# Another order of emission for the seven-product down steps of a spectral-filter and bilinear-GLU kernel

## The chip, the core and the metric

The kernel runs on one NeuronCore of a Trainium2 chip. The metric is the device time of one execution in microseconds (us). The engines are named as the profile names them: PE (TensorE matmul) with PEld (its weight loads), DVE (VectorE), ACT (ScalarE), POOL (GpSimd) and SP, whose queue issues most DMAs. Each engine works through its own list of instructions in order and waits on semaphores for the others.

## The reference

```python
x = A_x                                            # 1 x 2048 x 640
h = x + irfft2(rfft2(layernorm(x)) * (w_r + 1j * w_i))
z = layernorm(h)
g = z @ w_gate; u = z @ w_up                       # 640 x 1728 each
h2 = h + (g * u) @ w_down                          # 1728 x 640
```

All values are fp32. The change touches only the last two lines.

## The kernel before

Every fp32 operand of a matmul is split into a high part (a rounded copy, made on ACT) and a low part (the difference, made on DVE or POOL), and a product is three matmuls: high by high, high by low, low by high. Each engine's order is the order in which the code emits instructions; nothing reorders them.

The first part of the kernel (to about 190 us) is the spectral filter. The GLU part then runs over two blocks of 1024 tokens. The 1728 columns of the gate and up weights are cut into 14 chunks; a down step `p` takes two chunks. In a block, step 6 comes first (the last two chunks, computed plainly by `gu` and `gate_parts`), then steps 0 to 5. At the start of block 1 the normalised tokens are turned by PE transposes (`transp` for tiles 8 to 15, `fifth` for the last 128 columns of four tiles at once), and between them the last down step of block 0 is finished (`down`).

Steps 0 to 5 run `strassen` once for each of their two chunks. I call the two calls of a step its first and its second pass. A pass forms the gate and up products of one chunk by seven block products instead of eight: `product` issues groups of three matmuls (`triple`) into the PSUM banks `p11`, `acc_a` and `p53` (buffers `e` in the profile; there are four, used in turn). Partial results are copied out by ACT (`p1`, `u2`, `m5`) while PE works at another bank, and an accumulation onto `acc_a` or `p53` has to wait until its copy is done. Two quadrants of the gate product come out: `h[0](p53, m5)` and, at the end, `h[1](acc_a, p1)`.

In block 1, steps 0 to 4 are "mixed": their down product is also formed by seven block products. For it the quadrants of both passes are added and subtracted into seven operands, `unit(0)` to `unit(6)`, each with a high part (`high_of`, ACT) and a low part (`low_of`, DVE, for units 3 and 4 POOL). `mixed_first` makes units 2 and 3 at the end of the first pass, `mixed_second` units 0, 4, 5, 1 and 6 at the end of the second. `pending` is a list of such pieces that are put off, and `flush` emits them. `load_mixed` loads the down weights and gives three pieces: high parts of the plain weights; their low parts and the weight sums on POOL; and high and low parts of the sums (`third`, which is `wdn[2]`).

`mixed_down` turns the seven down products of step `p` into 16 stages, which are woven into the first pass of step `p + 1`: `tick` emits one stage after each group of three matmuls, from `p11` on. I call such a pass woven (its list `fine` is not empty; there are five, of steps 1 to 5). The stages of two token tiles alternate:

```python
k == 0:  unit 2 x b11                         then one DVE add of that bank (both line 911)
k == 1:  unit 4 x t2 onto it, unit 5 x t1     then one DVE add of both banks (line 904)
k == 2:  unit 3 x t3, unit 6 x b22            the same
else:    unit 0 x t4, unit 1 x b21            the same
```

`ahead` holds four pieces that prepare the gate and up weights of the next pass: `copies` (line 702 on ACT, 703 on POOL), `sums` (706 to 709 on POOL), `high` (714 on ACT) and `low` (719 on POOL). When `low` is through, the next load into the staging tile `raw` can start. `side` holds pieces by place, which `at(n)` emits.

Of the kernel before, what the change touches and what calls it, by code (L numbers as in the profile page):

```python
# [13 lines left out]
AF = mybir.ActivationFunctionType  # L14
OP = mybir.AluOpType
# [31 lines left out]
def tile_spectral_glu(ctx: ExitStack, tc: tile.TileContext, x, wf, wgu, wlast, wdown, wdlast,  # L47
                      cc, ci, fmain, frem, imain, irem, mm, out):
    nc = tc.nc
# [6 lines left out]
    tt, act = nc.vector.tensor_tensor, nc.scalar.activation  # L56
# [160 lines left out]
    def at(base, t):  # L217
        return view(base, 4 * t, [[64, 32], [1, 4]])
# [370 lines left out]
    def transp(t):  # L589
        turn_mm(t)  # L590
        turn_hi(t)
        turn_lo(t)
# [134 lines left out]
    def high_of(u, src):  # L727
        act(unit(u)[0], src, AF.Copy)  # L728

    def low_of(u, src, engine=nc.vector):  # L730
        hi, lo = unit(u)
        engine.tensor_tensor(lo, src, f32(hi), op=OP.subtract)  # L732
# [45 lines left out]
    def issue(job, parts=(0, 1)):  # L778
        for i in parts:
            for h in job[i]:  # L780
                h()

    EX, RAW, pending = {}, {}, []

    def flush():
        while pending:
            pending.pop(0)()

    def raw(k):
        RAW[k] = work.tile([P, 512], F32, tag="raw", name="rawh", bufs=3)  # L790
        return RAW[k]
# [10 lines left out]
    def mixed_first():  # L802
        def h1(ps, m):
            tt(raw(21), ps, m, op=OP.mult)
            return lambda: None

        def h0(ps, m):
            tt(ps, ps, m, op=OP.mult)
            high_of(2, ps)
            tt(raw(3), ps, RAW[21], op=OP.subtract)  # L810
            high_of(3, RAW[3])

            def rest():
                low_of(2, ps)
                low_of(3, RAW[3], nc.gpsimd)
            return rest
        return h1, h0

    def mixed_second():
        def h1(ps, m):  # L820
            tt(ps, ps, m, op=OP.mult)
            high_of(0, ps)
            tt(raw(2), ps, RAW[3], op=OP.subtract)
            high_of(4, RAW[2])

            def rest():
                low_of(0, ps)
                low_of(4, RAW[2], nc.gpsimd)
                tt(ps, ps, RAW[21], op=OP.add)
                high_of(5, ps)  # L830
                pending.append(lambda: low_of(5, ps))
            return rest

        def h0(ps, m):
            tt(ps, ps, m, op=OP.mult)
            high_of(1, ps)
            flush()

            def rest():
                low_of(1, ps)  # L840
                tt(ps, ps, RAW[2], op=OP.subtract)
                high_of(6, ps)
                pending.append(lambda: low_of(6, ps))
            return rest
        return h1, h0

    def load_mixed(p):
# [79 lines left out]
    def strassen(c, blk, h, ahead, downs, side, fine=()):  # L927
        wa, ws = W[c]
        fine = list(fine)

        def some(n):
            for _ in range(n):
                if downs:
                    downs.pop(0)()
                    pop(1)

        def at(n):
            for f in side.get(n, ()):
                f()

        def tick():
            if fine:
                fine.pop(0)()

        b11, b21, b22 = ([operand(sb, k + i) for i in range(2)] for sb, k in ((0, 0), (0, 2), (1, 2)))
        t1, t2 = ([(TJ["12"][:, 0, m, k], TJ["12"][:, 1, m, k]) for k in range(2)] for m in range(2))
        t4 = [operand(1, k) for k in range(2)]
        b5 = [operand(sb, 4) for sb in range(2)]
        p11, acc_a, p53 = single(), single(), single()

        def product(o, w, a, ms, extra=(), start=True, tick=tick):
            triple(o, [(w, a + P * i, m) for i, m in enumerate(ms)] + list(extra), start, tick)

        product(acc_a, wa, 384, b11, tick=None)
        p1, u2, m5 = (wk([P, 512], n) for n in ("p1", "u2", "m5"))
        act(p1, acc_a, AF.Copy)  # L956
        at(0)
        product(p11, wa, 0, b21, [(wa, 256, b5[0])])
        if ahead:
            ahead[0]()  # L960
            ahead[1]()
        flush()
        tt(p1, p11, p1, op=OP.add)
        at(1)
        product(acc_a, ws, 0, t2, start=False)
        act(u2, acc_a, AF.Copy)
        if ahead and fine:
            ahead[2]()
            ahead[3]()
            ahead = None  # L970
        product(p53, ws, 256, t1, [(wa, 896, b5[1])])
        act(m5, p53, AF.Copy)  # L972
        some(2)
        at(2)
        product(acc_a, ws, 640, [(t3[:, k, 0], t3[:, k, 1]) for k in range(2)], start=False)
        tt(m5, acc_a, m5, op=OP.add)  # L976
        some(1)
        product(p53, ws, 896, b22, [(ws, 512, b5[1])], start=False)
        tt(p53, p53, u2, op=OP.add)
        rest = h[0](p53, m5)  # L980
        at(3)
        some(2)
        rest()
        if ahead:
            ahead[2]()
            ahead[3]()
        product(acc_a, wa, 640, t4, [(wa, 896, b5[0])], start=False)
        while fine:
            tick()
        some(1)  # L990
        rest = h[1](acc_a, p1)
        at(4)
        some(1)
        rest()
        some(8)
        at(5)
# [5 lines left out]
    for n, (blk, p) in enumerate(steps):  # L1002
        if p == 6:
            s13, s12 = count % 3, (count + 1) % 3
            if blk == 0:
                load_raw(0)
                copies, sums, high, low = prep(0, blk, nc.vector)
                TJ["12"] = home("qr", [P, 2, 2, 2, 512], "t12", F32R)
                t1s = [t12(j) for j in range(4)]
                for j in range(4):  # L1010
                    t1s[j][0]()
                copies()
                t1s[0][1]()
                late()
                t1s[1][1]()
                t1s[2][1]()
                fifth((5, 6, 7))
                t1s[3][1]()
                late = gate_parts(NC - 2, 0, s12)
                sums()  # L1020
                high()
                for j in range(4):
                    t_rest(j)
                hi, lo = t34(0)
                hi()
                low()
                lo()
                late()
                gu(NC - 1, 1)
                wdn = load_d(p)  # L1030
                gate_parts(NC - 1, 1, s13)()
            else:
                copies, sums, high, low = prep(0, blk)
                js = [4, 5, 6, 7, 0, 1, 2, 3]
                for j in range(8):
                    transp(8 + j)
                    if j % 4 == 3:
                        fifth(range(5 + j, 9 + j))
                    if j >= 1:
                        down(*prev, js[j - 1], True)  # L1040
                    if j == 3:
                        copies()
                        sums()
                    if j == 5:
                        high()
                        low()
                down(*prev, js[7], True)
                gu(NC - 1, 0)
                gate_parts(NC - 1, 0, s13)()
                gu(NC - 2, 0)  # L1050
                TJ["12"] = home("qr", [P, 2, 2, 2, 512], "t12", F32R)
                t1s = [t12(j) for j in range(4)]
                late = gate_parts(NC - 2, 0, s12)
                for j in range(4):
                    t1s[j][0]()
                    t_rest(j)
                late()
                gu(NC - 1, 1)
                for j in range(4):
                    t1s[j][1]()  # L1060
                wdn = load_d(p)
                late = gate_parts(NC - 1, 1, s13)
                hi, lo = t34(0)
                hi()
                late()
                lo()
            gu(NC - 2, 1)
            gate_parts(NC - 2, 1, s12)()
            issue(wdn)
            prev = (blk, 6, [(2 * k, 2 * k + 1) for k in (s12, s13)])  # L1070
            count += 2
            load_raw(1)
            if blk == 0:
                fs, cs = scale_shift(range(8, 16), None)
                fill.extend(fs + cs)
            continue
# [14 lines left out]
        for ci in range(2):  # L1091
# [1 line left out]
            side = {}  # L1093
            ahead = None
            if c == 0:
                side[0] = t34(1)
            if c < 11:
                ahead = prep(c + 1, blk)
                side[5] = [lambda c=c: load_raw(c + 2)] if c < 10 else []
            if ci == 0 and mixed:  # L1100
                side[2] = [wdn[0], wdn[1]]
                side[4] = [wdn[2]]
            elif ci == 0:
                side[3] = [lambda wdn=wdn: issue(wdn)]
            if c == 11 and blk == 0:
# [148 lines left out]
```

## Time and profile before

| what | value |
|---|---|
| median of 3 runs | 747.57 us (746.79 to 748.72) |
| profiled execution | 750.67 us, its span 748.5 us, mean granted PE clock 0.981 |
| PE busy | 708.4 us (95%) |
| DVE, ACT, POOL busy | 446.5, 293.0 and 334.9 us (60%, 39%, 45%) |
| woven passes begin (their first stage) | 513.63, 556.57, 601.65, 646.28, 690.89 us |

The span runs from the first to the last instruction; 2.2 us of the execution lie around it. In the timeline a row is: start, duration (of all that are merged in it), engine, line, operation, out<-in, how many, and in brackets how long the engine had been idle and what released it.

### The profile page before, as it was taken

To read this page: it belongs to the slowest core of one execution; us is meant where nothing else is said; L and a number is where in the kernel's file an instruction comes from. 1 tells how busy PE (TensorE), PEld (TensorE's weight loads), DVE (VectorE), ACT (ScalarE), POOL (GpSimd) and SP (SyncE) were. 2 spreads that over 40 slices of the span, in tenths; PEclk is the share of its full clock that TensorE was granted. 3 is DMA by queue.
4 is the path that set the end of the run, shared out by engine and by line. 5 is a ranking of instruction groups with operands and counts; after the bars stand their busy time and mean duration, and the time that the engine had idled before them with its cause. 6 is when DMAs were issued, how large, how long until landed. Compare 5 with 4: busy or idle time off the path is not lost.

```text
span 748.5 us, 10074 instructions
## 1 busy us (share of the span) xinstructions
PE 708.4 (95%) x3832; PEld 621.3 (83%) x3832; DVE 446.5 (60%) x787; ACT 293.0 (39%) x554; POOL 334.9 (45%) x310
## 2 busy tenths in 40 slices
PE   7899998999999999999999999999979888898898
PEld 6788997887788989898888888897968777797887
DVE  7968886897964444454434475655645365564554
ACT  4756665375443223232232473533142232324220
POOL 3301114331165545545464521475776656575610
PEclk9999999999999999999999999999999999899999
DMA  9305663001201211121112122212103020110203
GB/s 338 150 8 191 224 214 127 1 1 44 96 3 36 71 35 71 36 71 36 70 36 89 39 102 100 77 36 70 36 0 106 1 71 35 56 51 0 71 0 141
DMA packets 20927, 55.04 MB, mean 74 GB/s; under 512 B 2320, under 2 KB 6928, under 8 KB 20880
## 3 DMA queue, kind: packets, MB, share of 16 engines
q1 hardware_dynamic: 20304, 52.70, 20.2%
q0 software_dynamic: 288, 1.48, 0.6%
q8 instruction: 30, 0.49, 0.3%
q10 hardware_dynamic: 288, 0.23, 0.1%
q14 instruction: 17, 0.14, 0.1%
HBM read 49.16 MB, written 5.24 MB: 73 GB/s over the span
## 4 chain that ended last, share of the span: by engine, by line
PE 72%; DVE 17%; ACT 6%; issue 2%; DMA 1%; POOL 1%; DVEq 0%; ACTq 0%
PE e L82 36%; PE y L82 24%; PE re L82 2%; PE im L82 2%; PE u L341 2%; PE eo L82 2%; ACT ht L728 2%; DVE fold L191 1%; ACT wst L714 1%; DVE fold L196 1%; DVE ht L732 1%; PE im L391 1%; PE im L390 1%; PE ir L382 1%; ACT wd L860 1%
## 5 line engine op out<-in xcount | busy, mean ns | idle before, releaser
L82 PE MATMUL e<-xt,wst 128*128 128x512 f32 x864 | 214.7, 391 | 2.6 <-ACT m L972 1.4
L82 PEld LDWEIGHTS e<-xt,wst 128*128 128x128 f32 x864 | 159.1, 188 | 32.7 <-ACT m L972 1.7
L82 PE MATMUL y<-wd,ht 128*128 128x320 f32 x1048 | 175.3, 315 | 11.4 <-DVE x L911 9.3
L82 PEld LDWEIGHTS y<-wd,ht 128*128 128x128 f32 x1048 | 164.2, 192 | 22.0 <-issue 11.4
L703 POOL TENSOR_TENSOR wst<-raw,wst 128x1024 fp32r<-128x1024 f32 x24 | 59.8, 2492 | 108.0 <-ACT wst L702 108.0
L508 DVE TENSOR_TENSOR x<-y,x 128x640 f32<-128x640 f32 x79 | 64.9, 823 | 68.0 <-PE y L82 67.8
L728 ACT ACTIVATE ht<-e 128x512 fp32r<-128x512 f32 x47 | 28.1, 598 | 176.6 <-DVE e L796 100.0
L82 PE MATMUL e<-t,wst 128*128 128x512 f32 x288 | 80.3, 424 | 9.0 <-ACT p L956 9.0
L82 PEld LDWEIGHTS e<-t,wst 128*128 128x128 f32 x288 | 58.2, 207 | 22.4 <-ACT p L956 11.4
L719 POOL TENSOR_TENSOR wst<-raw,wst 128x896 fp32r<-128x896 f32 (+1 forms) x46 | 64.8, 1432 | 23.6 <-ACT wst L714 23.6
L904 DVE TENSOR_TENSOR x<-y,x 128x640 f32<-128x640 f32 x60 | 49.4, 824 | 38.6 <-PE y L82 38.6
L464 POOL TENSOR_TENSOR wd<-draw,wd 128x640 fp32r<-128x640 f32 x18 | 28.0, 1579 | 66.7 <-ACT wd L463 66.7
L976 DVE TENSOR_TENSOR m<-e,m 128x512 f32<-128x512 f32 x24 | 16.5, 689 | 59.1 <-PE e L82 57.8
L702 ACT ACTIVATE wst<-raw 128x1024 fp32r<-128x1024 f32 x24 | 25.4, 1060 | 48.4 <-DMA raw<-in_wgu_dram 48.4
L82 PE MATMUL e<-xt,wdir 128*128 128x512 f32 x180 | 41.9, 392 | 1.1 <-DVE q L494 1.1
L732 DVE TENSOR_TENSOR ht<-e,ht 128x512 fp32r<-128x512 f32 x47 | 32.2, 684 | 17.3 <-ACT ht L728 16.9
L714 ACT ACTIVATE wst<-raw 128x896 fp32r<-128x896 f32 (+1 forms) x48 | 30.0, 676 | 29.2 <-POOL raw L708 28.4
L82 PEld LDWEIGHTS e<-xt,wdir 128*128 128x128 f32 x180 | 33.4, 188 | 8.3 <-ACT xt L547 1.3
L82 PE MATMUL e<-ht,wst 128*128 128x512 f32 x144 | 37.7, 391 | 0.0
L207 PE MATMUL im<-bits,fold 128*128 128x128 f32 x192 | 29.9, 292 | 6.7 <-DVE fold L196 2.3
L409 POOL CAST qr<-bits 1x128 fp32r<-1x128 f32 x16 | 4.5, 281 | 68.0 <-DVE qr L406 68.0
L207 PEld LDWEIGHTS im<-bits,fold 128*128 128x128 f32 x192 | 24.6, 193 | 11.4 <-DVE fold L196 5.6
(210 smaller groups left out, 1167.4 us busy)
## 6 DMA issues: line engine op xcount, KB each, us to landing
raw<-in_wgu_dram SPq DMA_DIRECT2D x24, 640.0 KB, 3.9
wts<-in_wf_dram SPq DMA_DIRECT2D x16, 644.0 KB, 4.0
draw<-in_wdown_dram SPq DMA_DIRECT2D x24, 320.0 KB, 4.6
x<-in_x_dram SPq DMA_DIRECT2D x16, 320.5 KB, 6.0
out_dram<-x SPq DMA_DIRECT2D x15, 320.0 KB, 2.2
bits<-in_mm_dram SPq DMA_DIRECT2D x32, 128.0 KB, 4.0
raw<-in_wgu_dram SPq DMA_DIRECT2D x4, 320.0 KB, 4.0
draw<-in_wdlast_dram SPq DMA_DIRECT2D x4, 320.0 KB, 2.9
```

Source lines behind the costliest of these rows:

```text
L82: nc.tensor.matmul(o, l, r, start=start, stop=stop, skip_group_check=True)
L207: nc.tensor.matmul(pm[:, k * P:(k + 1) * P], l, c, start=n == 0, stop=n == len(ls) - 1)
L464: los.append(lambda r=r, a=a, b=b: engine.tensor_tensor(w[:, 1, a:b], r, f32(w[:, 0, a:b]), op=OP.subtract))
L508: tt(xv, ps[:, :, 0:320], xv, op=OP.add)
L702: act(wa[:, 0], stage[:, 0:1024], AF.Copy)
L703: nc.gpsimd.tensor_tensor(wa[:, 1], stage[:, 0:1024], f32(wa[:, 0]), op=OP.subtract)
L714: act(ws[:, 0, o:o + b - a], stage[:, a:b], AF.Copy)
L719: ptt(ws[:, 1, o:o + b - a], stage[:, a:b], f32(ws[:, 0, o:o + b - a]), op=OP.subtract)
L728: act(unit(u)[0], src, AF.Copy)
L732: engine.tensor_tensor(lo, src, f32(hi), op=OP.subtract)
L904: tt(xv, PQ[q][:, :, 0:320], xv, op=OP.add)
L976: tt(m5, acc_a, m5, op=OP.add)
```

## The change

The sums of gate products, the low parts and the weight sums are emitted in another order:

- `flush(n)` emits at most n pieces instead of all.
- `mixed_first`: only the multiplication and the subtraction for unit 3 stand at the end of the first pass. The two high and two low parts of units 2 and 3 are put off into the second pass: one behind its `p1` copy, two between `copies` and `sums`, one behind `sums`.
- `mixed_second`: the subtraction for unit 4 goes ahead of the high part of unit 0; the sum of unit 5 goes behind the multiplication of the second quadrant; the low parts of units 5, 1 and 6 and the sum of unit 6 are put off. In the woven pass one such piece follows each stage.
- In a woven pass, `copies` and `sums` come behind the `u2` copy (before: behind `p11`), `high` and `low` behind the `m5` copy (before: ahead of it).
- The high and low parts of the weight sums (`wdn[2]`) come ahead of the last quadrant's work of the first pass (`at(6)`), before behind it (`at(4)`).
- The down weights of step 6 are split inside the next pass, behind its `p1` copy, before ahead of that pass.
- At the start of block 1, `fifth` comes behind the down step that it stood ahead of, twice.

```diff
-    def flush():
-        while pending:
-            pending.pop(0)()
+    def flush(n=8):
+        for h in pending[:n]:
+            h()
+        del pending[:n]
...
         def h0(ps, m):                       # mixed_first
             tt(ps, ps, m, op=OP.mult)
-            high_of(2, ps)
             tt(raw(3), ps, RAW[21], op=OP.subtract)
-            high_of(3, RAW[3])
-            def rest():
-                low_of(2, ps)
-                low_of(3, RAW[3], nc.gpsimd)
-            return rest
+            pending.extend([
+                lambda: high_of(2, ps),
+                lambda: low_of(2, ps),
+                lambda: high_of(3, RAW[3]),
+                lambda: low_of(3, RAW[3], nc.gpsimd)])
+            return lambda: None
...
         def h1(ps, m):                       # mixed_second
             tt(ps, ps, m, op=OP.mult)
+            tt(raw(2), ps, RAW[3], op=OP.subtract)
             high_of(0, ps)
-            tt(raw(2), ps, RAW[3], op=OP.subtract)
             high_of(4, RAW[2])
-            def rest():
+            low_of(4, RAW[2], nc.gpsimd)
+            def fifth_sum():
                 low_of(0, ps)
-                low_of(4, RAW[2], nc.gpsimd)
                 tt(ps, ps, RAW[21], op=OP.add)
                 high_of(5, ps)
                 pending.append(lambda: low_of(5, ps))
-            return rest
+            held.append(fifth_sum)
+            return lambda: None
...
         def h0(ps, m):                       # mixed_second
             tt(ps, ps, m, op=OP.mult)
             high_of(1, ps)
-            flush()
-            def rest():
-                low_of(1, ps)
+            held.pop()()
+            def sixth_sum():
                 tt(ps, ps, RAW[2], op=OP.subtract)
                 high_of(6, ps)
-                pending.append(lambda: low_of(6, ps))
-            return rest
+            pending.extend([lambda: low_of(1, ps), sixth_sum, lambda: low_of(6, ps)])
+            return lambda: None
...
             if fine:                         # tick
                 fine.pop(0)()
+                flush(1)
...
+        woven = bool(fine)                   # strassen
         product(acc_a, wa, 384, b11, tick=None)
...
         at(0)
+        if not woven:
+            flush(1)
         product(p11, wa, 0, b21, [(wa, 256, b5[0])])
-        if ahead:
+        if ahead and not woven:
             ahead[0]()
+            flush(2)
             ahead[1]()
-        flush()
+            flush()
         tt(p1, p11, p1, op=OP.add)
         at(1)
         product(acc_a, ws, 0, t2, start=False)
         act(u2, acc_a, AF.Copy)
-        if ahead and fine:
+        flush()
+        if ahead and woven:
+            ahead[0]()
+            ahead[1]()
+        product(p53, ws, 256, t1, [(wa, 896, b5[1])])
+        act(m5, p53, AF.Copy)
+        if ahead and woven:
             ahead[2]()
             ahead[3]()
-            ahead = None
-        product(p53, ws, 256, t1, [(wa, 896, b5[1])])
-        act(m5, p53, AF.Copy)
...
         some(1)
+        at(6)
         rest = h[1](acc_a, p1)
...
                     transp(8 + j)            # start of block 1
+                    if j >= 1:
+                        down(*prev, js[j - 1], True)
                     if j % 4 == 3:
                         fifth(range(5 + j, 9 + j))
-                    if j >= 1:
-                        down(*prev, js[j - 1], True)
...
-            issue(wdn)
+            first_wd = wdn
...
-                side[0] = t34(1)
+                side[0] = [*t34(1), lambda j=first_wd: issue(j)]
...
-                side[4] = [wdn[2]]
+                side[6] = [wdn[2]]
```

On ACT, at the seam between the first and the second pass of step 2 (`p` is the copy `p1` of the second pass, `wd` the high parts of the weight sums, line 728 a high part of a unit), there stood:

```order
L860 ACTIVATE ex_4066<-draw_4364 128x640
L728 ACTIVATE ht_1714<-e_4368 128x512
L728 ACTIVATE ht_1714<-rawh_4561 128x512
L860 ACTIVATE wd_4362<-draw_4363 128x640
L860 ACTIVATE wd_4362<-draw_4364 128x640
L956 ACTIVATE p1_4580<-e_4572 128x512
L702 ACTIVATE wst_4593<-raw_1814 128x1024
```

and now stands:

```order
L862 ACTIVATE ex_4062<-draw_4360 128x640
L862 ACTIVATE wd_4358<-draw_4359 128x640
L862 ACTIVATE wd_4358<-draw_4360 128x640
L960 ACTIVATE p1_4576<-e_4568 128x512
L728 ACTIVATE ht_1714<-e_4364 128x512
L702 ACTIVATE wst_4590<-raw_1814 128x1024
L728 ACTIVATE ht_1714<-rawh_4564 128x512
```

Both high parts of the units moved behind `p1`, and the weight sums' high parts are now ahead of everything that waits for the last quadrant.

On DVE, at the seam between the second pass of step 2 and the woven first pass of step 3 (835, now 838, is the second quadrant's multiplication; 829, now 831, the sum of unit 5; 841, now 843, that of unit 6; 911 and 904, now 913 and 906, the stages' adds; 963, now 970, the `p1` sum), there stood:

```order
L823 TENSOR_TENSOR rawh_4637<-e_4573,rawh_4561 128x512
L732 TENSOR_TENSOR ht_1714<-e_4573,ht_1714 128x512
L829 TENSOR_TENSOR e_4573<-e_4573,rawh_4527 128x512
L835 TENSOR_TENSOR e_4572<-e_4572,p1_4580 128x512
L732 TENSOR_TENSOR ht_1714<-e_4573,ht_1714 128x512
L732 TENSOR_TENSOR ht_1714<-e_4572,ht_1714 128x512
L841 TENSOR_TENSOR e_4572<-e_4572,rawh_4637 128x512
L911 TENSOR_TENSOR x1_67<-y_4685,x1_67 128x320
L911 TENSOR_TENSOR x1_67<-y_4693,x1_67 128x320
L904 TENSOR_TENSOR x1_67<-y_4685,x1_67 128x2x320
L732 TENSOR_TENSOR ex_4066<-e_4572,ex_4066 128x512
L963 TENSOR_TENSOR p1_4678<-e_4669,p1_4678 128x512
```

and now stands:

```order
L838 TENSOR_TENSOR e_4568<-e_4568,p1_4576 128x512
L732 TENSOR_TENSOR ht_1714<-e_4569,ht_1714 128x512
L831 TENSOR_TENSOR e_4569<-e_4569,rawh_4527 128x512
L913 TENSOR_TENSOR x1_67<-y_4681,x1_67 128x320
L732 TENSOR_TENSOR ht_1714<-e_4569,ht_1714 128x512
L913 TENSOR_TENSOR x1_67<-y_4690,x1_67 128x320
L732 TENSOR_TENSOR ht_1714<-e_4568,ht_1714 128x512
L906 TENSOR_TENSOR x1_67<-y_4681,x1_67 128x2x320
L843 TENSOR_TENSOR e_4568<-e_4568,rawh_4636 128x512
L970 TENSOR_TENSOR p1_4674<-e_4665,p1_4674 128x512
L906 TENSOR_TENSOR x1_67<-y_4690,x1_67 128x2x320
L732 TENSOR_TENSOR ex_4062<-e_4568,ex_4062 128x512
```

The first stage's add moved ahead of three operations that make units 5, 1 and 6, and the low part of unit 6 (`ex`) moved behind the `p1` sum and one more stage's add.

On PE, at the start of block 1 (537 is a transpose of `transp`, 568 one of `fifth`, `y` a down step), the difference is:

```order
 L537 MATMUL e<-ident,zt 128x128 x4
+L82 MATMUL y<-wd,ht 128x320 x12
 L568 MATMUL e<-ident,zt 128x128 x4
-L82 MATMUL y<-wd,ht 128x320 x12
 L537 MATMUL e<-ident,zt 128x128 x4
 L82 MATMUL y<-wd,ht 128x320 x12
```

One down step of 12 matmuls moved ahead of the four transposes.

More of the change, by code (lines that the diff above doesn't have):

```diff
@@ L808, in h0 @@
             tt(ps, ps, m, op=OP.mult)
-            high_of(2, ps)
             tt(raw(3), ps, RAW[21], op=OP.subtract)
-            high_of(3, RAW[3])
-            def rest():
-                low_of(2, ps)
-                low_of(3, RAW[3], nc.gpsimd)
-            return rest
+            pending.extend([
[4 more added lines that the diff above has]
+            return lambda: None
         return h1, h0
     def mixed_second():
+        held = []
         def h1(ps, m):
             tt(ps, ps, m, op=OP.mult)
+            tt(raw(2), ps, RAW[3], op=OP.subtract)
             high_of(0, ps)
-            tt(raw(2), ps, RAW[3], op=OP.subtract)
             high_of(4, RAW[2])
-            def rest():
+            low_of(4, RAW[2], nc.gpsimd)
+            def fifth_sum():
                 low_of(0, ps)
-                low_of(4, RAW[2], nc.gpsimd)
                 tt(ps, ps, RAW[21], op=OP.add)
@@ L983, in strassen @@
         rest()
-        if ahead:
+        if ahead and not woven:
             ahead[2]()
```

## The prediction

> **What bounds the kernel now.** The first view is the page's list of busy times:
>
> ```profile
> PE 708.4 (95%) x3832; PEld 621.3 (83%) x3832; DVE 446.5 (60%) x787; ACT 293.0 (39%) x554; POOL 334.9 (45%) x310
> ```
>
> PE is the bound almost everywhere, and the change takes no matmul away. So there is something to win only where PE waits or where its matmuls run slowly. The second view is the list of waits in the stretch from 505 to 720 us, where the passes with mixed down steps lie (waiter, releaser: us in all, times, longest):
>
> ```profile
> PE y L82 <- DVE x L911: 9.3, 5, 1.9
> PE e L82 <- ACT p L956: 8.1, 4, 2.3
> PE e L82 <- ACT m L972: 1.4, 1, 1.4
> ```
>
> Ten waits, 18.8 us: one at the start of each of the five woven passes, one in each of four second passes, and one more. The third view is the granted clock behind them. Of ten stretches of 5 us, one behind each wait, seven read 0.66 and three read 1.00; the first, an undisturbed one and the last are these (length, PE busy, clock, DMA share, GB/s):
>
> ```profile
> 517.00:522.00 5.00, 4.13 (x16) 0.66 0.57 193
> 560.00:565.00 5.00, 4.11 (x25) 1.00 0.54 189
> 695.00:700.00 5.00, 4.79 (x19) 0.66 0.72 244
> ```
>
> A dip costs 5 x (1 - 0.66) = 1.7 us of PE work. Two of the longer waits have none behind them:
>
> ```profile
> 545.55 3.02 PE L82 MATMUL e<-t,wst 128*128 128x512 f32 x12 [1.96 <-ACT p L956]
> 560.89 1.12 PE L82 MATMUL y<-wd,ht 128*128 128x320 f32 x6 [1.88 <-DVE x L911]
> ```
>
> In time spent the waits cost 18.8 us and the seven dips 12 us.
>
> **The wait of the second passes.** The timeline of the seam at 630 us:
>
> ```profile
> 628.10 3.60 PE L82 MATMUL e<-xt,wst 128*128 128x512 f32 x15
> 629.83 0.60 ACT L728 ACTIVATE ht<-e 128x512 fp32r<-128x512 f32 x1 [10.67 <-DVE e L808]
> 631.78 1.35 ACT L860 ACTIVATE wd<-draw 128x640 fp32r<-128x640 f32 x2
> 633.03 0.57 ACT L956 ACTIVATE p<-e 128x512 f32<-128x512 f32 x1
> 633.66 1.62 PE L82 MATMUL e<-t,wst 128*128 128x512 f32 x4 [1.96 <-ACT p L956]
> 603.39 2.78 POOL L719 TENSOR_TENSOR wst<-raw,wst 128x896 fp32r<-128x896 f32 x2 [0.72 <-ACT wst L714]
> 625.50 0.88 POOL L875 TENSOR_TENSOR draw<-draw 128x320 f32<-128x320 f32 x1
> ```
>
> The bank that `p1` copies is full after 6 of the 15 matmuls at 628.10, at about 629.5. ACT reaches the copy only at 633.03: it stood idle for 10.67 us, then had two unit copies (the second waits for DVE) and 1.35 us of weight sums before it. The change puts the weight sums ahead, into the idle time, and the two unit copies behind. What is late next? The weight sums' high parts wait for the POOL sums, which end at 626.38 (last row). By that row they run to 627.8, `p1` to 628.4. PE will come earlier, though: in the new order I let the woven pass begin at the same 601.65 (below). Its 28 products and 15 groups take 22.8 us (0.44 and 0.70 each, below), `p1`'s and `p11`'s matmuls 3.4, and 0.7 of waiting stays, so PE wants the copy at 628.6. The POOL chain moves forward as well: from the end of line 719 at 606.17 to the end of 875 is 20.2 us, and 719 now starts 0.9 us earlier, at about 602.5 (its ACT copy is no longer behind a unit copy). The sums end at 625.5, `p1` at 627.5: 1.1 us to spare. Term: -8.1 us for the four waits. The put-off unit copies delay `u2`, but that is needed 5 us later; units 2 and 3 are needed in the next pass. The POOL low part of unit 3 now stands behind `sums`; nothing waits for it there. The third wait of the list, on `m5`, arises because ACT has line 714 ahead of `m5` and waits for POOL in it; `m5` is now ahead of it. Term: -1.4. Line 702, which still stands ahead of `m5` and waits for a load, ends 2 us before `m5`'s bank is full by the same count, from 719's end, 4 us of load and 1 us of copy.
>
> **The wait of the woven passes.** The seam at 600 us, and below it three rows that give the price of a group of three (0.70 from the start of the first row to that of the second) and of a stage's product (0.44):
>
> ```profile
> 595.53 6.28 PE L82 MATMUL e<-xt,wst 128*128 128x512 f32 x27
> 599.94 0.69 DVE L823 TENSOR_TENSOR rawh<-e,rawh 128x512 f32<-128x512 f32 x1 [0.74 <-ACT ht L728]
> 601.65 0.60 PE L82 MATMUL y<-ex,ht 128*128 128x320 f32 x3
> 601.75 0.69 DVE L835 TENSOR_TENSOR e<-e,p 128x512 f32<-128x512 f32 x1
> 602.37 1.25 ACT L714 ACTIVATE wst<-raw 128x896 fp32r<-128x896 f32 x2
> 605.34 0.88 DVE L911 TENSOR_TENSOR x<-y,x 128x320 f32<-128x320 f32 x2
> 605.97 1.15 PE L82 MATMUL y<-wd,ht 128*128 128x320 f32 x6 [1.88 <-DVE x L911]
> 614.77 0.86 PE L82 MATMUL e<-xt,wst 128*128 128x512 f32 x3
> 615.47 0.60 PE L82 MATMUL y<-wd,ht 128*128 128x320 f32 x3
> 615.91 0.61 PE L82 MATMUL y<-ex,ht 128*128 128x320 f32 x3
> ```
>
> The first stage starts at 601.65 and its add could start at 602.3, but DVE gets to line 911 at 605.34, behind the multiplication, two low parts and the sum of unit 6, and PE's third stage, due at 601.65 + 2 x 0.44 + 2 x 0.70 = 603.93, waits until 605.97.
>
> In the new order the last quadrant's bank is full after 18 of the 27 matmuls, at 599.8, and DVE multiplies at 599.9. With 0.6 to 0.75 us from one DVE operation to the next: low part of unit 0 at 600.65 (its ACT copy runs from 600.0), sum of unit 5 at 601.3, first stage's add 602.3 to 602.8. ACT, after the copies of units 0 and 4, has 714 from 601.1, then units 1 and 5, to 603.3; DVE makes unit 5's low part by 604.0, then the second stage's add and unit 1's low part by 605.0. PE's third stage at 603.93 finds the first add done and needs the low part of unit 5 with its sixth matmul, at about 604.7. So this wait goes. The next candidate is the fifth stage, which needs unit 6. DVE goes on: third stage's add 605.0, sum of unit 6 605.75, `p1` sum 606.35, fourth stage's add 606.95 to 607.75 (0.8 for two banks), low part of unit 6 at 607.7 to 608.4. PE reaches the fifth stage at 603.93 + 0.88 + 0.70 + 0.88 + 0.70 = 607.09 and wants that low part with its last matmul, at 607.8. It waits for 0.7 us. So of 1.88 us, 0.7 is handed on: term -(9.3 - 5 x 0.7) = -5.8. The bounds: 0 kept (-9.3) if DVE starts its row 0.7 us sooner, and all kept (0) if every step of this DVE row slips by 0.1 to 0.2 us.
>
> **The dips.** No wait of 1.4 us or less has a dip behind it in these rows, seven of nine waits of 1.8 to 2.3 us have one. With waits of 0.7 and 0 us left, I take all seven to go: -12.0. The bounds are -12.0 and 0.
>
> [...]
>
> **The start of block 1.** Its timeline before:
>
> ```profile
> 440.05 0.60 PE L568 MATMUL e<-ident,zt 128*128 128x128 f32 x4
> 441.68 2.02 PE L82 MATMUL y<-wd,ht 128*128 128x320 f32 x12 [1.03 <-DVE x L508]
> 441.92 0.69 ACT L570 ACTIVATE xt<-e 128x512 fp32r<-128x512 f32 x1
> 442.40 1.15 ACT L702 ACTIVATE wst<-raw 128x1024 fp32r<-128x1024 f32 x1
> 443.53 0.60 PE L537 MATMUL e<-ident,zt 128*128 128x128 f32 x4
> 448.82 1.26 ACT L714 ACTIVATE wst<-raw 128x896 fp32r<-128x896 f32 x2 [1.85 <-POOL raw L708]
> 449.98 0.58 ACT L547 ACTIVATE xt<-e 128x512 fp32r<-128x512 f32 x1
> 450.60 0.69 DVE L555 TENSOR_TENSOR xt<-e,xt 128x512 fp32r<-128x512 f32 x1 [1.39 <-ACT xt L547]
> 452.86 1.76 PEld L82 LDWEIGHTS y<-wd,ht 128*128 128x128 f32 x12 [0.20 <-DVE x L508]
> ```
>
> This edit costs time. `fifth` ran in the shadow of PE's wait for a free `y` buffer. Now the down step takes PE at 441.68 and the four transposes run where the next ones stood, 443.53 to 444.13. ACT's copy of them moves from 441.92 to 444.17: 2.25 us. Behind it on ACT, in order, stands line 702, behind that POOL's 703 to 708, which 714 waits for, behind 714 the copy 547, and behind it on DVE 555 and, in turn, the add that frees the buffer for the last down step, for which PE already waits 0.20. Every link is a wait now or close to it, so PE's last down step moves by about 2.25 us. Term: +2.25. Bounds: +0.4 (only the transposes out of PE's shadow) and +4 (an idle time of 2 us, and a dip behind it).
>
> **The weights of step 6.** At the start of block 0:
>
> ```profile
> 205.73 1.35 ACT L463 ACTIVATE wd<-draw 128x640 fp32r<-128x640 f32 x2
> 206.99 0.59 ACT L956 ACTIVATE p<-e 128x512 f32<-128x512 f32 x1
> 207.62 3.02 PE L82 MATMUL e<-t,wst 128*128 128x512 f32 x12 [0.89 <-ACT p L956]
> ```
>
> `p1` no longer stands behind the weights; PE saves its 0.89 us of waiting. Its twin in block 1 waited less, and I count 0.9 for both. The down weights become ready 1.5 us later, when the first down step of that pass just begins: the high parts by 208.6, POOL's low parts by 211.1, about when PE asks for the second half. Bounds: -1.2 and +0.5.
>
> **The sum.** -8.1 - 1.4 - 5.8 - 12.0 + 2.25 - 0.9 = -26. The profiled execution took 750.67 us, so the same execution would take 724.7. The median of the runs is 3.1 us lower than that execution. If that is two dips fewer (2 x 1.7), it has no part in the new kernel, and 724.7 stands; if the profiled execution is simply longer by so much, it is 721.6. I take 723, between them. A second count, by periods, from the first and the last of the five first stages:
>
> ```profile
> 513.63 0.60 PE L82 MATMUL y<-ex,ht 128*128 128x320 f32 x3
> 690.89 0.60 PE L82 MATMUL y<-ex,ht 128*128 128x320 f32 x3
> ```
>
> That is 44.3 us a period now. In the new order it is 22.8, 63 matmuls of 0.23 us (27 in 6.1, first row of the seam at 600) and 0.7 of waiting, 37.9. Four periods save 25.7, the last woven pass 1.2 and a dip: 28.6, where the terms above have 27.3.
>
> **The rivals.**
> - The wait is passed on in full: units 5 and 6 come as late as the add came before, and each woven pass keeps 1.9 us and its dip. For it speaks that DVE has 12 operations in a row here and ACT three between two of them. Price: 5 x 1.2 of waiting and 4 of the 5 dips, 6.8: 736.
> - The clock dips aren't caused by these waits. For it: the two waits with no dip. Against: seven of nine. 723 + 12 = 735.
> - `p1` now waits for POOL. The high parts of the weight sums stand ahead of it and of everything that ACT does for the last quadrant. If POOL's 20.2 us grow by over 1.1, PE waits again; 3 us more give 4 x 1.9 and 4 dips: 737.
> - Slower, the same place: with PE's passes shorter, POOL's chain (load, copies, sums, low parts) would have to set the period. By the sum above a period is 37.9 us; slower than before needs `p1` 7 us later than I have it, four times, that is sums that end at 633 instead of 625.5. At 9 us it is 755. POOL is busy for 45% of the span, so I give it little.
> - The start of block 1 costs only 0.4 and the fifth stage doesn't wait: 723 - 1.9 - 3.5 = 718.
>
> **How the numbers follow.** The forecast has 0.60 (719 to 728 by its own bounds), the lower case 0.15, the passed-on wait 0.10, dips that stay 0.05, `p1` behind POOL 0.07, slower 0.02, no change in all 0.01. From 716 to 735 lie the forecast, the lower case but for a part of it, and the nearer parts of the three cases at 735 to 737, some 0.8. Faster by over 0.3% (2.2 us, about what can be told from no change) are all but the last two: 0.97; within 0.3%: 0.01; slower: 0.02.
>
> **What will show it.** Right: no wait of PE on `p1` in the second passes, on the first stage's add or on `m5`; a wait of 0.5 to 1 us of PE on a low part of unit 6 (DVE line 732) in the fifth stage of each woven pass; clock 1.00 from 505 us on; first stages 38 us apart; PE idle for 2 us ahead of the last down step at the start of block 1, with ACT's line 570 at 444.2. Wrong: waits of 1.8 us or more anywhere in the woven passes, the clock at 0.66 behind shorter ones, or ACT idle ahead of line 862 for POOL with PE waiting behind it.

## The result, and the profile after

The changed kernel takes 721.62 us (median of 4 runs, 720.85 to 722.89), the kernel before 748.14 (4 runs, 746.79 to 749.6). The ratio is 0.9647, with a 95% interval of 0.9621 to 0.9673: 3.5% faster. The forecast was 723. The profiled execution takes 720.87 us, its span is 719.1. The page's busy times, and the list of PE's waits from 480 to 700 us (waiter, releaser: us in all, times, longest):

```profile
PE 694.4 (97%) x3832; PEld 611.6 (85%) x3832; DVE 445.0 (62%) x787; ACT 294.0 (41%) x554; POOL 333.8 (46%) x310
```

```profile
PE y L82 <- DVE ex L732: 2.2, 5, 0.4
PE y L82 <- DVE x L906: 0.5, 1, 0.5
```

The ten waits are gone. In their place stand five of 0.44 us, on the low part of unit 6 in the fifth stage of each woven pass. The one of 0.5 us stood in the kernel before too (there on DVE's line 904). The clock of the same stretch, after and before (start and end, length, PE busy, clock, DMA share, GB/s):

```profile
505.00:700.00 195.00, 192.31 (x985) 1.00 0.14 48
```

```profile
505.00:715.00 210.00, 191.11 (x922) 0.94 0.13 44
```

No dip is left there. The seam of a second pass, in the timeline:

```profile
612.30 3.60 PE L82 MATMUL e<-xt,wst 128*128 128x512 f32 x15
612.69 0.74 ACT L862 ACTIVATE wd<-draw 128x640 fp32r<-128x640 f32 x1 [1.17 <-POOL draw L877]
613.89 0.60 ACT L960 ACTIVATE p<-e 128x512 f32<-128x512 f32 x1 [0.46 <-PE e L82]
614.69 0.60 ACT L728 ACTIVATE ht<-e 128x512 fp32r<-128x512 f32 x1 [0.20 <-DVE rawh L810]
615.74 2.88 PE L82 MATMUL e<-t,wst 128*128 128x512 f32 x12
```

`p1` now waits for PE, not for ACT's own queue, and ends at 614.49, 1.25 us ahead of the matmul that needs it. The seam of a woven pass:

```profile
588.83 0.60 PE L82 MATMUL y<-ex,ht 128*128 128x320 f32 x3
589.47 0.49 DVE L913 TENSOR_TENSOR x<-y,x 128x320 f32<-128x320 f32 x1 [0.40 <-PE y L82]
591.10 1.04 PE L82 MATMUL y<-wd,ht 128*128 128x320 f32 x6
594.11 0.82 DVE L906 TENSOR_TENSOR x<-y,x 128x640 f32<-128x640 f32 x1
594.67 0.46 PE L82 MATMUL y<-ex 128*128 128x320 f32 x2
594.84 0.68 DVE L732 TENSOR_TENSOR ex<-e,ex 128x512 fp32r<-128x512 f32 x1
595.58 0.41 PE L82 MATMUL y<-ex 128*128 128x320 f32 x1 [0.44 <-DVE ex L732]
```

The first stage's add runs 0.64 us after the stage starts, the third stage 2.27 us after it without a wait, and the last matmul of the fifth stage waits for the low part of unit 6. And the start of block 1:

```profile
439.37 2.02 PE L82 MATMUL y<-wd,ht 128*128 128x320 f32 x12 [1.47 <-DVE x L508]
441.23 0.60 PE L568 MATMUL e<-ident,zt 128*128 128x128 f32 x4
441.86 0.60 ACT L570 ACTIVATE xt<-e 128x512 fp32r<-128x512 f32 x1 [2.05 <-PE e L568]
448.64 1.26 ACT L714 ACTIVATE wst<-raw 128x896 fp32r<-128x896 f32 x2 [3.55 <-POOL raw L708]
452.69 2.03 PE L82 MATMUL y<-wd,ht 128*128 128x320 f32 x12 [1.64 <-DVE x L508]
454.55 5.63 PE L82 MATMUL e<-xt,wdir 128*128 128x512 f32 x24
```

From the start of the first of these down steps to the first matmul of the gate products it is 454.55 - 439.37 = 15.18 us here; before it was 454.72 - 441.68 = 13.04.

### The profile page after: what moved, and what is told of

The parts are those of the page before. It is cut to its first block, busy times and chain, and to the rows that moved or that the text cites. A ratio compares the mean times of both kernels' runs of the same rounds, so it can differ in the third digit from the quotient of the medians.

```text
span 719.1 us, 10059 instructions
## 1 busy us (share of the span) xinstructions
PE 694.4 (97%) x3832; PEld 611.6 (85%) x3832; DVE 445.0 (62%) x787; ACT 294.0 (41%) x554; POOL 333.8 (46%) x310
## 4 chain that ended last, share of the span: by engine, by line
PE 78%; DVE 13%; issue 4%; ACT 3%; POOL 1%; DMA 1%; DVEq 0%; POOLq 0%; ACTq 0%
PE e L82 42%; PE y L82 24%; PE re L82 2%; PE im L82 2%; PE u L341 2%; PE eo L82 2%; DVE fold L191 1%; DVE x L906 1%; DVE fold L196 1%; PE im L391 1%; PE im L390 1%; PE ir L382 1%; ACT zt L525 1%; DVE x L510 1%; DVE bits L215 1%
## 5 line engine op out<-in xcount | busy, mean ns | idle before, releaser
L82 PE MATMUL y<-wd,ht 128*128 128x320 f32 x1048 | 171.3, 310 | 4.3 <-DVE x L508 3.1
L82 PEld LDWEIGHTS y<-wd,ht 128*128 128x128 f32 x1048 | 160.8, 188 | 13.3 <-DVE x L508 3.6
L703 POOL TENSOR_TENSOR wst<-raw,wst 128x1024 fp32r<-128x1024 f32 x24 | 57.9, 2412 | 113.2 <-ACT wst L702 108.0
L82 PE MATMUL e<-t,wst 128*128 128x512 f32 x288 | 71.9, 390 | 0.0
L82 PEld LDWEIGHTS e<-t,wst 128*128 128x128 f32 x288 | 53.3, 188 | 9.7
```

What stands on the lines that cost most here:

```text
L82: nc.tensor.matmul(o, l, r, start=start, stop=stop, skip_group_check=True)
L703: nc.gpsimd.tensor_tensor(wa[:, 1], stage[:, 0:1024], f32(wa[:, 0]), op=OP.subtract)
```

## The experiments

All times are medians; the kernel before was run beside each group of them (747.39, 749.38 and 748.87 us).

**The start of block 1 put back.**

```diff
-                    if j >= 1:
-                        down(*prev, js[j - 1], True)
                     if j % 4 == 3:
                         fifth(range(5 + j, 9 + j))
+                    if j >= 1:
+                        down(*prev, js[j - 1], True)
```

> The changed kernel with the transposes of the last columns (fifth) put back ahead of the down step at the start of block 1. Theory (that edit costs time, by ACT's copy behind them moving 2.2 us): PE's wait of 1.64 us ahead of the last down step falls to about 0.2 and the time to 719.5 us, 2.1 under the changed kernel's 721.6. Rival (its wait is only moved, nothing behind it is late): 721.6, within 0.5 us.

718.88 us, ratio 0.962 (0.9595 to 0.9645). Its interval overlaps the changed kernel's, so the time alone doesn't settle 2 us; the timeline does:

```profile
439.26 2.02 PE L82 MATMUL y<-wd,ht 128*128 128x320 f32 x12 [1.00 <-DVE x L508]
448.50 3.95 PE L82 MATMUL y<-wd,ht 128*128 128x320 f32 x24
452.28 4.04 PE L82 MATMUL e<-xt,wdir 128*128 128x512 f32 x17
```

The stretch takes 13.02 us again, and the last two down steps run on without a wait. This edit of the change costs 2.1 us.

**`mixed_second` put back** (with its `flush` inside `h0`, and `low_of(0)`, `low_of(5)`, `low_of(1)` and both sums ahead of the first stage again).

> The changed kernel with mixed_second as it was before (the sums of units 5 and 6 and the low parts of units 0, 5 and 1 stand ahead of the first stage's add again; the rest stays). Theory (these operations on DVE are the woven passes' wait, and such waits cause the clock's dips): five waits of 1.9 us of PE on line 913 instead of five of 0.4 on unit 6, and three to five dips of 1.7: 721.6 + 7.3 + 5 to 8.5 = 734 to 738 us. Rival (the dips have another cause): the waits come back, no dips, 729.

729.29 us, ratio 0.9779 (0.9733 to 0.9826). The five waits are back, but the clock fell behind only one of them in the profiled execution; three runs took 729.2 to 729.3, and one, with a mean clock of 0.983 instead of 0.993, took 735.44. The first and the last of the five, the waits and the clock behind them:

```profile
517.61 1.12 PE L82 MATMUL y<-wd,ht 128*128 128x320 f32 x6 [1.81 <-DVE x L911]
674.17 1.76 PE L82 MATMUL y<-wd,ht 128*128 128x320 f32 x6 [1.81 <-DVE x L911]
```

```profile
517.00:522.00 5.00, 4.39 (x26) 1.00 0.62 203
674.00:679.00 5.00, 4.83 (x19) 0.66 0.72 245
```

So the order of `mixed_second` makes the woven passes' wait, as predicted, but a wait of this length doesn't always bring a dip.

**The pieces for the next weights put back.**

```diff
         product(p11, wa, 0, b21, [(wa, 256, b5[0])])
+        if ahead and woven:
+            ahead[0]()
+            ahead[1]()
...
         act(u2, acc_a, AF.Copy)
         flush()
         if ahead and woven:
-            ahead[0]()
-            ahead[1]()
+            ahead[2]()
+            ahead[3]()
```

> The changed kernel with the four pieces for the next pass's weights where they stood in the woven passes (copies and sums behind p11, high and low ahead of m5). Theory (line 714 waits for POOL's sums and holds m5 up; before, it showed only once because four woven passes were slowed by dips): PE waits about 2 us on m5 in each of the five woven passes, and dips follow most of them: 721.6 + 10 + 5 to 8.5 = 737 to 740 us; without dips 732. Rival (the place of these pieces matters only in the one pass where it showed, 1.4 us): 723.

731.77 us, ratio 0.9784 (0.9755 to 0.9814):

```profile
PE e L82 <- ACT m L982: 7.6, 5, 1.8
PE y L82 <- DVE ex L732: 2.2, 5, 0.4
```

A wait on `m5` in each of the five woven passes, 1.3 to 1.8 us, and a dip behind the longest alone (clock 0.66 from 531 to 536 us, 1.00 from 540 to 700). That is the theory without its dips. In the kernel before, this wait showed once because a dip made PE late to it in the other passes: there, and in the two experiments below that start from that kernel (the weight sums alone, the put-off alone), it shows in exactly those woven passes behind whose first wait the clock stayed at 1.00 (one, two and three of the five).

**The weight sums alone**, on the kernel before (`side[6]` with its `at(6)`).

> The kernel before with one edit of the change: the high parts of the weight sums ahead of the last quadrant's work; the two unit copies stay ahead of p1. Theory (both stand in p1's way, each does part): PE's wait on p1 in the second passes falls from 2.0 to about 0.7 us, too short for a dip: 4 x 1.3 + 3 x 1.7 = 10 less than before, about 737 us. Rival (the weight sums alone are the wait): 8.1 + 5 = 13 less, 734. Rival (the unit copies alone are): as before, 747.

738.72 us, ratio 0.9858 (0.9843 to 0.9873). The first and the last of the four waits on `p1`, which are 0.71, 0.99, 0.71 and 0.71 us:

```profile
542.88 3.02 PE L82 MATMUL e<-t,wst 128*128 128x512 f32 x12 [0.71 <-ACT p L956]
668.23 3.01 PE L82 MATMUL e<-t,wst 128*128 128x512 f32 x12 [0.71 <-ACT p L956]
```

12 matmuls in 3.0 us is the full clock (1.00 from 542 to 547 us, behind the first). The theory holds: PE's waiting on `p1` falls from 8.1 to 3.1 us. The wait on `m5` shows in two passes instead of one (2.5 us), which takes a little of it back.

**The put-off alone**, on the kernel before (only the new `mixed_first`).

> The kernel before with the other edit alone: the high and low parts of units 2 and 3 put off behind p1 (all of them behind p11); the weight sums stay where they were. Since nothing of the last quadrant is left on ACT ahead of the weight sums, ACT can make them in its idle time without being moved. Theory: no wait on p1 is left, its dips go too: 8.1 + 3 x 1.7 = 13 less, about 734 us. Rival (the weight sums need their move): p1 still about 1.3 us late, 4 x 0.7 + 5 = 8 less, 739.

735.21 us, ratio 0.9812 (0.9795 to 0.9828). PE's waits from 480 to 730 us:

```profile
PE y L82 <- DVE x L910: 9.1, 5, 1.8
PE e L82 <- ACT m L971: 3.5, 3, 1.4
```

No wait on `p1` is left although the weight sums weren't moved. The other way round no run is needed: once the unit copies are put off, only two DVE operations lie between `at(6)` and `at(4)`, so the changed kernel with `wdn[2]` back at `at(4)` has the same order on every engine as with it at `at(6)` (only the numbers of some buffers differ). Either edit shortens the wait; the put-off alone removes it, and behind the put-off the move does nothing.

**The weights of step 6 put back** (`issue(wdn)` ahead of the next pass).

> The changed kernel with the down weights of step 6 split ahead of the next pass again, as before. Theory: PE waits 0.9 us on p1 in the first pass of block 0 and 0.2 in that of block 1, against 0.2 on the weights now: 722.3 us, 0.7 to 0.9 over the changed kernel. Rival (it changes nothing): 721.6.

722.2 us (721.62 to 723.36), ratio 0.9637 (0.9623 to 0.9652): by the time this can't be told from no change. In the timeline PE's wait of block 0 is back:

```profile
206.87 3.03 PE L82 MATMUL e<-t,wst 128*128 128x512 f32 x12 [0.89 <-ACT p L960]
```

**A wait of chosen length.** Idle copies on ACT ahead of `p1`, in five second passes:

```diff
+        if pending and not woven:
+            for _ in range(3):               # 6, 9
+                act(idle, idle, AF.Copy)
         act(p1, acc_a, AF.Copy)
```

> The changed kernel with three idle copies of 512 columns on ACT (about 0.5 us from one to the next, 1.5 in all, onto a scratch tile) ahead of p1 in the five second passes that follow a mixed first pass. Theory (p1 has 1.2 us to spare there, of which ACT's idle 0.46 ahead of it makes 1.7): no wait of PE on p1, 721.6 us, within 0.5. Rival (p1 is as good as on PE's path): 5 x 1.5 = 7.5 more, 729.

> The same with six idle copies, 3 us. Theory (waits of about 1.4 us bring no dip): PE waits 1.3 to 1.5 us on p1 five times, clock 1.00 from 505 us on, 721.6 + 7 = 728 to 729 us. Rival (any wait can bring a dip): up to 5 x 1.7 more, 737.

> The same with nine idle copies, 4.5 us. Theory (a wait of PE of over half of some 3.4 us, the length of a dip, brings the clock down behind it): PE waits about 2.9 us five times, a dip of 1.7 us behind each: 721.6 + 14.5 + 8.5 = 744 to 745 us, and little scatter between runs. Rival (the dips have another cause than the waits): 736.

They measured 722.58, 735.69 and 747.58 us; ratios 0.9639 (0.9625 to 0.9654), 0.9837 (0.9814 to 0.9861) and 0.999 (0.9976 to 1.0005). A copy took 0.66 us (nine in 5.92), not 0.5, so six and nine made longer waits than I had chosen. Three made one wait of 0.44 us, so the time to spare ahead of PE's path is there; by what the copies take and what PE waits in the three kernels it is 1.5 to 2.3 us in four of the five passes. The first of the five has more: even with nine copies its `p1` ends at 503.54, and PE's matmul starts at 504.50 without a wait. Six made four waits; the first two, and the clock behind all four:

```profile
543.15 4.61 PE L82 MATMUL e<-t,wst 128*128 128x512 f32 x12 [2.24 <-ACT p L965]
584.73 3.01 PE L82 MATMUL e<-t,wst 128*128 128x512 f32 x12 [1.85 <-ACT p L965]
```

```profile
543.00:548.00 5.00, 4.84 (x14) 0.66 0.00 0
584.00:589.00 5.00, 4.27 (x19) 1.00 0.00 0
624.00:629.00 5.00, 4.31 (x12) 0.66 0.00 0
666.00:671.00 5.00, 4.69 (x21) 1.00 0.00 0
```

The other two waits were 1.91 (dip) and 1.87 (none). With nine copies the four waits are 3.7 to 4.1 us, and each has a dip; the first and the last:

```profile
546.53 5.49 PE L82 MATMUL e<-t,wst 128*128 128x512 f32 x12 [4.08 <-ACT p L965]
679.61 5.49 PE L82 MATMUL e<-t,wst 128*128 128x512 f32 x12 [3.67 <-ACT p L965]
```

Twelve matmuls take 2.6 us more than at the full clock (5.28 against 2.72 from the first to what follows them). Four waits, 15.5 us, and four times 2.6 on top of 721.6 are 747.5, near the measured median; the profiled execution, 749.55, has a dip of 1.7 us at 125 to 129 us besides. All four waits of this length brought the dip. That a wait of over half of a dip's 3.4 us is enough, the theory here, isn't shown: of the 29 waits of 1.8 to 2.3 us counted below, 13 had no dip.

**A version that keeps the gain and drops the loss.** The start of block 1 as before, and the `p1` sum of the woven passes behind the put-off pieces:

```diff
-        tt(p1, p11, p1, op=OP.add)
+        if not woven:
+            tt(p1, p11, p1, op=OP.add)
...
         flush()
+        if woven:
+            tt(p1, p11, p1, op=OP.add)
```

> The changed kernel with fifth back as before at the start of block 1, and in the woven passes the p1 sum put behind the low part of unit 6 on DVE. Theory (both are what the change leaves or makes worse): the last wait in the woven passes falls from 0.44 to about 0.1 us, 5 x 0.35 = 1.7 less, and 2.1 less at the start of block 1: 717.8 us. Rival (the fourth stage's add, not the p1 sum, holds the low part of unit 6 up): 719.5.

716.88 us, ratio 0.9591 (0.9567 to 0.9615). No matmul of the woven passes waits for unit 6 any more; its weight loads wait 1.8 us in all, 3.5 before:

```profile
PEld y L82 <- DVE ex L732: 1.8, 5, 0.4
```

It is the fastest of the kernels here, 4.1% under the one before. Its slowest run (718.62) lies just under the fastest (718.67) of the kernel with only the start of block 1 put back.

## Why the prediction was right, point by point

- **Second passes, -8.1: right, with one reason too many.** The waits are gone, and 1.25 us are to spare where 1.1 was forecast. The forecast let ACT's weight sums set the start of `p1`; they end earlier, and ACT is idle for 0.46 us until PE has filled the bank. The step that credits the move of the weight sums failed: the put-off alone takes the wait away, and beside it the move changes nothing.
- **`m5`, -1.4: right as it stood in the profile, too small as a part.** Without this edit the changed kernel waits 7.6 us there and takes 10 us more. In the kernel before, the dips of four woven passes covered it, and the experiments with fewer dips show it in each woven pass that has none.
- **Woven passes, -5.8: -7.1.** 9.3 us of waits became 2.2, where I kept 5 x 0.7. The place was right (unit 6, fifth stage, last matmul). The low part of unit 6 ended 6.7 us after the first stage's start, as counted (594.84 + 0.68 - 588.83). The matmul that waits for it follows two that start at 594.67 and some 0.15 us apart, so it was due at 594.97 and came at 595.58: 0.6 us late, 0.7 by the count. Of that only 0.44 us shows as idle time of PE, since the two before it end at 595.13 (594.67 + 0.46); so the waits read 2.2 us and not 3.5.
- **Period, 37.9 us: 37.8** ((664.42 - 513.31) / 4, first stages).
- **The dips, -12.0: right in sum, too sure in the reason.** That the waits cause them is shown by the idle copies, and by the place of the dips: in the twelve profiled executions all 20 dips between 200 us and the last microseconds of the span stand behind a PE wait of 1.8 us or more (16 behind 1.8 to 2.3 us, four behind 3.7 to 4.1). But at 1.8 to 2.3 us the length alone doesn't decide whether a dip follows. Of the waits of this length in the profiled executions of the kernel before and of five experiments, 16 of 29 had one: 7 of 9 in the kernel before, 1 of 5, 1 of 1, 3 of 5, 2 of 5 and 2 of 4. The prediction took the 7 of 9 as the rule, so the two expectations that counted dips behind such waits (734 to 738, 737 to 740) came out too high. Its rows began at 505 us and left out a dip behind shorter waits, at 125 us (last section).
- **Start of block 1, +2.25: +2.1**, by the chain that was named. PE's wait ahead of the last down step is 1.64 us, where 2 was given.
- **Weights of step 6, -0.9: right by the timeline**, 0.89 us of waiting on `p1` for 0.2 on POOL's weights, and too small to be told by the medians (722.2 against 721.62).
- **The sum.** For the profiled execution -26 was forecast and -29.8 came (750.67 to 720.87). Of the 3.8 us between them up to 1.3 is the woven passes' wait, as idle time counts it; 1.7 is the dip at 125 to 129 us, far from the change, that the profiled execution before had and this one has not; 0.4 lies outside the spans (748.5 to 719.1 is 29.4); the last 0.4 isn't traced. The medians differ by 26.5. That 723 came within 1.4 us of the median is in part luck: it was the middle between two readings of the 3.1 us by which the profiled execution before exceeded its median, and what the terms left out is of the same size. Which reading was right can't be told, since only one execution of the kernel before was profiled.

Of the rivals, the passed-on wait was there in small (0.44 of 1.9 us). Dips that stay, `p1` behind POOL and a slower kernel did not come. The last one fell too: the start of block 1 cost 2.1 us where it had 0.4, and the fifth stage does wait.

## What to carry to other kernels

Where one engine is the bound and runs through short passes, look at what stands in the queues of the others ahead of the copy that frees its buffer: work that nobody needs yet can go behind it, here at no cost that the runs show, and which of two such pieces is in the way is told by moving one at a time. A wait that shows in one pass of five may be hidden in the other four by a slower bound (here 1.4 us in one pass, 7.6 in five), so count it for all when the bound gets faster. When transposes or other small pieces run in the shadow of a wait, moving the wait ahead of them takes the shadow away (here 2.1 us).

## What the runs showed of the hardware

From 200 us on, the clock fell behind no PE wait of 0.4 to 1.65 us in these profiles, behind about half of those of 1.8 to 2.3 us (16 of 29), and behind all four of 3.7 to 4.1 us. The same wait of 1.81 us in the same kernel (`mixed_second` put back) had a dip once and none four times. Two runs of that kernel took 729.29 and 735.44 us, at mean clocks of 0.993 and 0.983; at 1.7 us a dip that is between three and four dips, an estimate, since the slower one has no trace.

Ahead of 200 us, waits that are short but close together had dips too. All twelve profiled executions have three PE waits of some 0.65, 0.34 and 1.30 us between 121 and 125 us; three of them (the kernel before, the one with the pieces for the next weights put back and the one with nine copies) have a dip behind the last. From 120 to 130 us the clock is 0.83 in the second of these, and 1.00 in the kernel with `mixed_second` put back. Eight have a dip between 15 and 24 us too, behind waits of 0.3 to 1.0 us in a row. The wait at 125 us and the clock behind it in the kernel before, and the clock there in the changed kernel, which has the same waits:

```profile
124.92 1.80 PE L82 MATMUL eo<-tab,qm 128*128 128x161 f32 x8 [1.30 <-DVE qr L406]
```

```profile
124.00:129.50 5.50, 4.58 (x22) 0.69 0.00 0
```

```profile
120.00:130.00 10.00, 7.70 (x54) 1.00 0.02 7
```

So only waits of up to 1.65 us that stand alone are shown to go without a dip.

A dip behind a wait of some 2 us takes 1.7 us: 3.4 us at half clock (5 us at 0.66). Summed over stretches of 1 us, every dip of the twelve executions ahead of the last microseconds lasts 3.4 us or twice that, 6.8; in each of the eight of the kernel before, 1.70 to 1.71 us are lost. The four behind the waits of 3.7 to 4.1 us are of the longer kind (stretches of 10 us read 0.66 to 0.69, which is 6.2 to 6.8 us at half clock within them) and begin within the wait, so about 5.2 us are left behind it. One of them, of which the wait ends at 591.00:

```profile
590.00:591.00 1.00, 0.00 (x1) 0.50 0.00 0
595.00:596.00 1.00, 1.00 (x4) 0.50 0.00 0
596.00:597.00 1.00, 1.00 (x6) 0.87 0.00 0
```

What decides whether a dip follows a wait of some 2 us isn't shown: no run here moves a wait in time and changes nothing else. By the counts, half a dip is a fair price for such a wait in this kernel: an estimate, 16 / 29 x 1.7 = 0.9 us.
